# A recurrence's matmuls on one core: block-diagonal pairs of heads become single heads on parts of the array

## The chip, the core and the metric

The kernel runs on one core of a Trainium2 chip. A core has five engines with a queue of instructions each: TensorE (PE in the profile, its weight loads PEld), VectorE (DVE), ScalarE (ACT), GpSimd (POOL) and SyncE (SP), which here only issues transfers. The metric is the device time of one execution in microseconds; lower is better. All arithmetic of the recurrence is float32.

## The reference

```python
# r, k, v, w, a, b: (4 batches, 8 heads, 768 times, 40)
for t in range(S):
    y[:, :, t] = np.einsum('bhd,bhde->bhe', rt, state)
    Sa = np.einsum('bhde,bhe->bhd', state, at)
    state_decay = state * wt[:, :, None, :] - np.einsum('bhd,bhe->bhde', Sa, bt)
    state = state_decay + np.einsum('bhd,bhe->bhde', vt, kt)
x = y.transpose(0, 2, 1, 3).reshape(3072, 320)
x = (1 / (1 + exp(-(x @ w_gate))) * (x @ w_val)) @ w_out          # 320 -> 1536 -> 320
h = x @ w_in                                                      # 320 -> 2048
out = (h * (1 / (1 + exp(-1.702 * h)))) @ w_out2                  # 2048 -> 320
```

Each of the 32 pairs of batch and head has a state of 40 x 40. The two mixtures' weights come as 64-bit words that the kernel decodes on VectorE.

## The kernel before

The 768 times are cut into 24 chunks of C = 32, and a chunk into two halves: a half chunk h (48 of them) is one chunk's work for 16 of the 32 heads. Inside a chunk the recurrence becomes matrix products, with one triangular 32 x 32 inverse for each head; the state passes from one chunk to the next. Two threads, `chain(0)` and `chain(1)`, carry the two halves of the heads along.

Heads go in pairs on the 128 rows: a pair has D + D = 80 rows where dimensions lie on rows, and 32 + 32 where times do. A product for two heads at once needs one operand that is block diagonal, with zeros where one head's rows meet the other's columns. So several operands are written twice, each copy masked for one head:

- `fronts(h)`: running products of w (`wx`, `suf`), then `kb` (k and b scaled; four VectorE or GpSimd instructions, L673), `dd`, and a scaled in place (L705). `diagonal` writes a into `abd` as two masked copies on ScalarE (L743).
- `back(h)`: transposes of `kb` into `pt` (two blocks of four, L771), copied with masks to `kn` (L774); `pm`, the scores between a and k, b (L789). `nl` (L798) and `lk` (L804) are what lies below and above their diagonals. `nl` goes through memory to `solve`, which makes the inverse `tn` on GpSimd (for the first three chunks on VectorE).
- `inverses` and `later` mask `tn` and `lk` into `tb` (L886) and `lkb` (L952); `later` also has `pv` (L938), the scores between v and r.
- `chain`: `po` from the state `sd` (16 passes), copied to `xh`; `pr` from `lkb`, then from `abd` and `xh`; copied to `rs`; `pu` from `tb` and `rs`, masked into `vu` (L1041); `kn` times `vu` added into `po`; the new state through `xb` (L1051), the transposes `px` (L1057) and a ScalarE copy into `sd`. y is read out of `po` (L1076).

`mm` (L561) is a helper through which most matmuls go, so that rows of very different blocks have one line; their tiles' names tell them apart. A float32 matmul of the program is two passes, each with a weight load, in the trace; a transpose and the mixtures' matmuls (in a shortened float32, fp32r) are one.

The first mixture (`moe1`) takes 256 tokens at a time (`gv`, then `xa`), as soon as the chunks are stored, and fills TensorE between the blocks of the recurrence; the second (`ph`, `y`) follows when the recurrence and the first are over. Most transfers are issued by SP.

The order of the instructions on every engine is fixed when the program is built. A planner (`Plan`) steps threads that `yield` an engine and a cost in microseconds, and gives each engine's next place to the thread that could start first, ties by a key. "EITHER" work goes to VectorE or GpSimd, whichever it finds free sooner. On the chip each engine runs its list in that order, waiting on semaphores.

Of the kernel before, what the change touches and what calls it, by code (L numbers as in the profile page):

```python
# [9 lines left out]
F32 = mybir.dt.float32  # L10
# [10 lines left out]
R = 2 * D  # L21
# [9 lines left out]
C_ID, C_I2, C_HM80, C_HM128, C_STR, C_UM, C_LKM, C_NHM, C_SEL, C_END = 0, 128, 168, 170, 172, 204, 276, 340, 342, 374  # L31


def constants():
    k = np.zeros((128, C_END), np.float32)
    p = np.arange(128)
    k[p, C_ID + p] = 1.0
    k[p[:R], C_I2 + p[:R] % D] = 1.0
    for j in range(2):
        k[:R, C_HM80 + j] = p[:R] // D == j  # L40
        k[:R, C_NHM + j] = -k[:R, C_HM80 + j]
        k[:, C_HM128 + j] = (p // C) % 2 == j
    k[p, C_SEL + p % 32] = 1.0
    t = np.arange(C)
    k[:, C_STR : C_STR + C] = t[None, :] < (p % C)[:, None]
    later = (t[None, :] > (p % C)[:, None]).astype(np.float32)
    k[:, C_UM : C_UM + C] = later
    k[:, C_UM + C : C_UM + C + D] = 1.0
    for j in range(2):
        k[:, C_LKM + C * j : C_LKM + C * j + C] = later * k[:, C_HM128 + j : C_HM128 + j + 1]  # L50
    return k
# [11 lines left out]
def layout(inp):  # L63
# [4 lines left out]
    def heads_on_rows(x):  # L68

        y = x.reshape(2, 2, 4, 2, NCH, C, D)  # L70
        return np.ascontiguousarray(y.transpose(4, 0, 3, 6, 1, 2, 5)).reshape(2 * NCH, R, 8, C)

# [5 lines left out]
    def apart(x):  # L78
# [8 lines left out]
        "rt": heads_on_rows(inp["r"]),  # L87
        "vt": heads_on_rows(inp["v"]),
# [120 lines left out]
def program(ctx: ExitStack, tc: tile.TileContext, abkw, rt, vt, vn, cst, x2, x4, in_r, in_k, in_v, in_w, in_a, in_b, moe_w_gate,  # L209
# [18 lines left out]
    ident = k[:R, C_ID : C_ID + R]  # L228
    hm80 = k[:R, C_HM80 : C_HM80 + 2]
    nhm80 = k[:R, C_NHM : C_NHM + 2]  # L230
    hm128 = k[:, C_HM128 : C_HM128 + 2]
    strict = k[:, C_STR : C_STR + C]
    umask = k[:, C_UM : C_UM + C + D]
    lkm = k[:, C_LKM : C_LKM + 2 * C].rearrange("p (j t) -> p j t", j=2)
# [162 lines left out]
    xs_slots, gv_slots, xa_slots, xz_free = Slots(2), Slots(2), Slots(1), Event()  # L397
# [178 lines left out]
    sd = at.tile([R, 16, R], F32, name="sd")  # L576
    ring = 2
    r72s = [at.tile([R, 8, C + D], F32, name=f"r72_{i}") for i in range(ring)]
    vbds = [at.tile([R, 8, 2, C], F32, name=f"vbd_{i}") for i in range(ring)]
    for i in range(2):  # L580
        r72s.append(wpool.tile([R, 8, C + D], F32, tag=f"B{6 + 3 * i}", name="r72_0"))
        vbds.append(wpool.tile([R, 8, 2, C], F32, tag=f"B{7 + 3 * i}", name="vbd_0"))
# [15 lines left out]
    half, tns = {}, {}  # L598
    groups = [[c] for c in range(min(SINGLE, NCH))] + [[c, c + 1] for c in range(SINGLE, NCH, 2)]
# [3 lines left out]
    s_slots, nl_slots, u_slots, tn_slots, tb_slots, b_slots, po_slots = Slots(2), Slots(2), Slots(2), Slots(1), Slots(2), Slots(0), Slots(1)  # L603
    yt_slots, xh_slots, rs_slots = Slots(1), Slots(2), Slots(1)
    e_ab, e_front, e_diag, e_scored, e_stored, e_wc = ([Event() for _ in range(NH)] for _ in range(6))
    e_b, e_vu, e_tb, e_sd, e_y, e_rows = ([Event() for _ in range(NH)] for _ in range(6))
    e_lower, e_tn = ([Event() for _ in range(NCH)] for _ in range(2))
# [25 lines left out]
    def fronts():  # L633

        thread = plan.current
        for h in range(NH):
# [29 lines left out]

            kb = at.tile([R, 4, 4, 2, C], F32, tag="kb", name="kb", bufs=2)
            kbv = kb.rearrange("p g (o x) j t -> p g o x j t", o=2)

            def scaled(eng, x, src, o):  # L670
                sv, cv = (bass.AP(tensor=y.tensor, offset=y[:, o : o + 1].offset, ap=[list(y.ap[0]), [2 * y.ap[1][0], 4], [0, 2], [1, C]])
                          for y in (src, ws))
                eng.tensor_mul(kbv[:, :, o, x ^ o], sv, cv)  # L673
# [13 lines left out]
            on = yield "EITHER", 0.34, 0.12, None, 0.7  # L687
            if h < START:
                ad = wpool.tile([R, 24, C], F32, tag=f"X{8 + h}", name="ad0")
            else:  # L690
                ad = at.tile([R, 24, C], F32, tag="ad", name="ad")
            dd = ad[:, 16:]
# [4 lines left out]
            wc = at.tile([R, 8, 2], F32, tag="wc", name="wc", bufs=DEPTH)  # L697
            nc.vector.tensor_mul(wc, wx[:, :, C:E].broadcast_to([R, 8, 2]), hm80.unsqueeze(1).broadcast_to([R, 8, 2]))
# [5 lines left out]
            on = yield "EITHER", 0.34, None, None, 0.7  # L704
            either[on].tensor_mul(a, a, dd)  # L705
            plan.start(diagonal(h, a, ad), f_key(h), plan.done + plan.LATENCY)
            for o in range(2):
                on = yield "EITHER", 0.34, None, None, 0.7
                scaled(either[on], 1, b, o)
# [5 lines left out]
            plan.start(over(h), f_key(h))  # L715
            plan.start(back(h, kb, ad), f_key(h), plan.done + plan.LATENCY)

    def over(h):

        yield e_front[h]  # L720
        yield e_diag[h]
        plan.done = max(e_front[h].time, e_diag[h].time)
        if h >= START:
            plan.give(ab_slots)
        elif all(e.time is not None for e in e_diag[:START]):
            plan.set(w1ready[1])
# [4 lines left out]
    def kl_parts(kl):  # L731
        return kl[:, : 16 * D].rearrange("p (g j d) -> p g j d", g=8, j=2), kl[:, 16 * D :].rearrange("p (g t) -> p g t", g=4)

    def views(h, ad, kl):
        st = half[h]
        st["abd"], st["dd"] = ad[:, 0:16].rearrange("p (g j) t -> p g j t", j=2), ad[:, 16:]
        st["kn"], st["lk"] = kl_parts(kl)

    def diagonal(h, a, ad):
        abd = ad[:, 0:16].rearrange("p (g j) t -> p g j t", j=2)  # L740
        for j in range(2):
            yield "ACT", 0.4
            nc.scalar.activation(abd[:, :, j, :], a, AF.Copy, scale=nhm80[:, j : j + 1])  # L743
        plan.set(e_diag[h], plan.LATENCY)

    def back(h, kb, ad):
# [3 lines left out]
        abd = ad[:, 0:16].rearrange("p (g j) t -> p g j t", j=2)  # L750
        if h >= START:
            yield kl_slots
            kl = at.tile([128, 16 * D + 4 * C], F32, tag="kl", name="kl")
        else:
            kl = wpool.tile([128, 16 * D + 4 * C], F32, tag=f"X{12 + h}", name="kl0")
            views(h, ad, kl)
        kn, lk = kl_parts(kl)
        st["kl_d"] = drp.tile([128, 16 * D + 4 * C], F32, tag="kl_d", name="kl_d", bufs=DEPTH)
        st["ad_d"] = drp.tile([R, 24, C], F32, tag="ad_d", name="ad_d", bufs=DEPTH)
        rows_done = Event()  # L760

        def on_rows():

            for sb in range(2):
                yield s_slots
                yield "PE", 0.28
                pt = ps_s.tile([128, 4, 2, D], F32, tag="s", name="pt")
                for i in range(4):
                    gi = 4 * sb + i
                    src = kb[:, gi // 2, 2 * (gi % 2) : 2 * (gi % 2) + 2].rearrange("p x j t -> p (x j t)")  # L770
                    nc.tensor.transpose(pt[:, i].rearrange("p j e -> p (j e)"), src, ident)  # L771
                for j in range(2):
                    yield "ACT", 0.28
                    nc.scalar.activation(kn[:, 4 * sb : 4 * sb + 4, j, :], pt[:, :, j, :], AF.Copy, scale=hm128[:, j : j + 1])  # L774
                plan.give(s_slots)
            plan.set(rows_done)

        plan.start(on_rows(), f_key(h) + 0.5, plan.done + plan.LATENCY)
        yield e_diag[h]
        yield s_slots  # L780
        yield "PE", 0.62

        pm = ps_s.tile([128, 4, 2, C], F32, tag="s", name="pm")
        for g2 in range(4):
            for o in range(2):

                a0 = kb[:, g2, 3 * o, 0, :]
                rhs = bass.AP(tensor=a0.tensor, offset=a0.offset, ap=[list(a0.ap[0]), [64 if o == 0 else -64, 2], [1, C]])
                nc.tensor.matmul(pm[64 * o : 64 * o + 64, g2], lhsT=abd[:, 2 * g2 + o].rearrange("p j t -> p (j t)"), rhs=rhs,  # L789
                                 start=True, stop=True)  # L790
        if q == 0:
            yield nl_slots
            nls[c] = at.tile([128, 8, C], F32, tag="nl", name="nl", bufs=2)
# [3 lines left out]
        yield "DVE", 0.2, plan.LATENCY  # L797
        nc.vector.tensor_mul(nls[c][:, hs], pm[:, :, 1, :], strict.unsqueeze(1).broadcast_to([128, 4, C]))  # L798
        if q == 0:
            plan.set(e_lower_first[c])  # L800
        else:
            plan.start(scores_out(c), f_key(h) - 0.3, plan.done + plan.LATENCY)
        yield "DVE", 0.2
        nc.vector.transpose(out=lk, in_=pm[:, :, 0, :])  # L804
        plan.give(s_slots)
# [18 lines left out]
    def scores_out(c):  # L824
# [4 lines left out]
        nc.sync.dma_start(out=ldrs[cs][c - cs[0]].rearrange("g r s -> r g s"), in_=nls.pop(c))  # L829
# [7 lines left out]
    def solve(cs, ldr, eng):  # L837
# [32 lines left out]
        tn = at.tile([128, 8 * len(cs), C], F32, tag="tn", name="tn")  # L870
# [4 lines left out]

    def inverses():

        thread = plan.current
        for h in range(NH):
            thread.key = h - 0.2  # L880
            c, hb = h // 2, h % 2
            yield e_tn[c]
            yield tb_slots
# [667 lines left out]
```

## Time and profile before

| | |
|---|---|
| median of 3 runs | 1319.49 us (1317.58 to 1319.65) |
| profiled execution | 1315.4 us, its span on the core 1313.6 us |
| mean granted TensorE clock | 0.943 |
| busy: TensorE, its weight loads | 1194.1 us (91%), 1100.4 us (84%) |
| busy: VectorE, ScalarE, GpSimd | 865.2 us (66%), 536.1 us (41%), 456.7 us (35%) |
| transfers | 163.31 MB on SP's queue, 126 GB/s in the mean |

A busy share is a mean over stages with different limits, and each stage has to be read for itself. A granted clock of 1.0 is 2.4 GHz, 0.5 is 1.2 GHz; the profile shows the mean of a stretch. Times of rows count from the span's start. "TensorE busy" counts a pass from its start to the end that the profile models for it, so neighbouring passes overlap in it.

### The profile page before, as it was taken

The numbers are of one execution on the slowest core, as the hardware profiler recorded it, in microseconds if no ns is written. First come the engines' busy times: TensorE is split into PE (matmuls) and PEld (weight loads), VectorE is DVE, ScalarE is ACT, GpSimd is POOL, SyncE is SP. The second block draws the span as 40 slices with busy tenths as digits, with TensorE's granted clock in tenths as the row PEclk, the third lists the DMA queues.
The fourth block names the chain that finished last, engine by engine and source line by source line (L and its number), as shares of the span: only waits on it lengthen the run. The fifth ranks groups of instructions, "written<-read, shape, count | busy, mean of one in ns | idle before, by whom it ended". The sixth has DMA issues, their size and how long they took to land. (4 is left out here: it accounts for less than half of the span.)

```text
span 1313.6 us, 30246 instructions
## 1 busy us (share of the span) xinstructions
PE 1194.1 (91%) x11505; PEld 1100.4 (84%) x11505; DVE 865.2 (66%) x2298; ACT 536.1 (41%) x1354; POOL 456.7 (35%) x882
## 2 busy tenths in 40 slices
PE   4366885999999999999999999999999999999996
PEld 3355784889889898999899999999988798899995
DVE  8997897756476656566656444439998656556552
ACT  3233454234434344444344433337774243434332
POOL 3236487836371808181817270002341000000000
PEclk9975795699999999999999999999999999999999
DMA  6566776475646474656465543225533422222110
GB/s 166 139 175 170 178 211 174 134 174 146 158 115 175 128 178 132 167 143 174 136 135 163 121 127 86 73 58 153 150 107 97 114 87 55 88 59 79 45 43 23
DMA packets 245144, 165.31 MB, mean 126 GB/s; under 512 B 173504, under 2 KB 215680, under 8 KB 244992
## 3 DMA queue, kind: packets, MB, share of 16 engines
q1 hardware_dynamic: 244992, 163.31, 47.4%
q8 instruction: 93, 1.52, 0.5%
q14 instruction: 59, 0.48, 0.1%
HBM read 117.05 MB, written 46.20 MB: 124 GB/s over the span
## 5 line engine op out<-in xcount | busy, mean ns | idle before, releaser
L561 PE MATMUL gv<-xs,w1i 128*128 128x256 f32 x1728 | 271.2, 299 | 0.0
L561 PEld LDWEIGHTS gv<-xs,w1i 128*128 128x128 f32 x1728 | 228.9, 196 | 7.1
L561 PE MATMUL y<-w2o,g 128*128 128x320 f32 x1152 | 185.2, 309 | 3.8 <-DVE g L1308 2.3
L859 POOL TENSOR_TENSOR ut<-x,u 128x126 f32<-128x126 f32 (+27 forms) x341 | 158.4, 465 | 83.7 <-DMA x<-in_x_dram 50.2
L561 PEld LDWEIGHTS y<-w2o,g 128*128 128x128 f32 x1152 | 176.2, 188 | 12.7 <-DVE g L1308 3.1
L561 PE MATMUL xa<-g,w1o 128*128 128x256 f32 x1152 | 173.1, 288 | 2.2 <-DVE x L464 1.7
L561 PE MATMUL ph<-xs,w2i 128*128 128x512 f32 x672 | 172.5, 396 | 2.4 <-DVE gg L1300 2.4
L862 POOL TENSOR_TENSOR x<-x,ut 128x126 f32<-128x126 f32 (+27 forms) x341 | 148.4, 435 | 26.0
L561 PEld LDWEIGHTS xa<-g,w1o 128*128 128x128 f32 x1152 | 151.4, 192 | 4.6 <-DVE x L464 1.9
L561 PEld LDWEIGHTS ph<-xs,w2i 128*128 128x128 f32 x672 | 122.9, 189 | 25.6 <-DVE gg L1300 4.3
L506 DVE TENSOR_TENSOR sg<-gv,sg 128x256 f32<-128x256 f32 x144 | 60.3, 419 | 112.7 <-ACT sg L504 112.1
L504 ACT ACTIVATE sg<-gv 128x256 f32<-128x256 f32 x144 | 55.3, 384 | 174.3 <-PE gv L561 173.4
L1300 DVE TENSOR_TENSOR gg<-ph,sg 128x512 f32<-128x512 f32 x96 | 66.0, 688 | 52.9 <-ACT sg L1296 52.8
L1306 ACT CAST g<-gg 128x512 fp32r<-128x512 f32 x96 | 59.5, 620 | 96.1 <-DVE gg L1300 96.0
L1308 DVE TENSOR_TENSOR g<-gg,g 128x512 fp32r<-128x512 f32 x96 | 66.7, 695 | 43.5 <-ACT g L1306 43.3
L1296 ACT ACTIVATE sg<-ph 128x512 f32<-128x512 f32 x96 | 57.2, 596 | 92.8 <-PE ph L561 92.7
L511 ACT CAST g<-sg 128x256 fp32r<-128x256 f32 x144 | 58.1, 404 | 88.5 <-DVE sg L506 75.3
L774 ACT ACTIVATE kl<-pt,k 128x160 f32<-128x160 f32 x192 | 67.3, 391 | 53.2 <-PE pt L771 39.5
L673 DVE TENSOR_TENSOR kb<-ab,suf 80x256 f32<-80x256 f32 x158 | 81.9, 552 | 3.8 <-PE pt L771 3.8
L561 PE MATMUL gv<-xs,w1r 128*128 128x256 f32 x288 | 82.8, 307 | 0.0
L513 DVE TENSOR_TENSOR g<-sg,g 128x256 fp32r<-128x256 f32 x144 | 64.7, 449 | 21.7 <-ACT g L511 21.4
L771 PE MATMUL pt<-k,kb 80*128 80x80 f32 x384 | 54.1, 270 | 25.7 <-DVE kb L673 12.9
(123 smaller groups left out, 2056.9 us busy)
## 6 DMA issues: line engine op xcount, KB each, us to landing
kl_d<-kl SPq DMA_DIRECT2D x44, 384.0 KB
kl_l<-kl_d SPq DMA_DIRECT2D x44, 384.0 KB
ab<-in_abkw_dram SPq DMA_DIRECT2D x44, 322.8 KB
ad_d<-ad SPq DMA_DIRECT2D x44, 240.0 KB
ad_l<-ad_d SPq DMA_DIRECT2D x44, 240.0 KB
u<-ldr SPq DMA_DIRECT2D x20, 256.0 KB
w<-in_moe_w_out_dram SPq DMA_DIRECT2D x32, 160.0 KB
w<-in_moe_w_in_dram SPq DMA_DIRECT2D x32, 128.0 KB
```

The lines of the kernel that those rows point to most:

```text
L506: nc.vector.tensor_mul(gg, gv[:, 1, :], gg)
L511: nc.scalar.copy(out=g4[:, 0], in_=gg)
L513: nc.vector.tensor_sub(out=g4[:, 1], in0=gg, in1=g4[:, 0].bitcast(F32))
L561: nc.tensor.matmul(o, lhsT=w, rhs=x, start=start, stop=stop, skip_group_check=True)
L673: eng.tensor_mul(kbv[:, :, o, x ^ o], sv, cv)
L774: nc.scalar.activation(kn[:, 4 * sb : 4 * sb + 4, j, :], pt[:, :, j, :], AF.Copy, scale=hm128[:, j : j + 1])
L859: eng.tensor_mul(tv, x[:, :n, s : s + 1].broadcast_to([128, n, m]), u[:, s + 1 :, s].unsqueeze(1).broadcast_to([128, n, m]))
L862: eng.tensor_add(x[:, :n, s + 1 :], x[:, :n, s + 1 :], tv)
L1296: nc.scalar.activation(sg, ph, AF.Sigmoid, scale=1.702)
L1300: nc.vector.tensor_mul(gg, ph, sg)
L1306: nc.scalar.copy(out=g4[:, 0], in_=gg)
L1308: nc.vector.tensor_sub(out=g4[:, 1], in0=gg, in1=g4[:, 0].bitcast(F32))
```

## The change

Nothing is block diagonal any more. A head has 40 of 64 rows (J = 64; R = 112 rows hold a pair), and each product is one matmul for one head, on a part of the array that its rows and its columns name: 64 or 32 rows by 64 or 32 columns. Four heads that follow each other in the list `HEADS` lie on four different parts. The masked copies fall away: `abd`, `lkb`, `tb`, the four `kb` writes (now two), `diagonal`, `inverses`. `pt` and `px` are ordinary matmuls with an identity, not transposes; `px` lies in unused columns of `po`'s PSUM banks. `kn` times `vu` is added in two blocks, `added(0)` and `added(1)`, each for the rows of `vu` that are ready. `sd` holds 40 columns where it held 80, `kl` 448 where it held 768. The loads are padded from 80 to 112 rows. PSUM banks of `po` are cleared once at the start.

```diff
+J = 64
+R = 112
...
+    HEADS = [(2 * g2 + o, g2, o, j) for g2 in range(4) for o in range(2) for j in range(2)]
+
+    def dims(j):
+        return slice(J * j, J * j + D)
+
+    def times(o, j):
+        return slice(64 * o + C * j, 64 * o + C * j + C)
...
             def kb0():
-                for o in range(2):
-                    on = yield "EITHER", 0.34, None, None, 0.7
-                    scaled(either[on], 0, kk, o)
+                on = yield "EITHER", 0.45, None, None, 0.8
+                either[on].tensor_mul(kb[:, :, 0], kk, ws)
...
-            for sb in range(2):
-                yield s_slots
-                yield "PE", 0.28
-                pt = ps_s.tile([128, 4, 2, D], F32, tag="s", name="pt")
-                for i in range(4):
...
+            yield s_slots
+            yield "PE", 0.4
+            pt = ps_s.tile([128, 8, D], F32, tag="s", name="pt")
+            for gi, g2, o, j in HEADS:
+                for x in range(2):
+                    mm(pt[times(o ^ x, j), gi], kb[dims(j), gi, x], ident[j], True, True)
+            yield "ACT", 0.42
+            nc.scalar.copy(out=kn, in_=pt)
...
+        for gi, g2, o, j in HEADS:
+            mm(pm[times(o, j), g2], an[dims(j), gi], kb[dims(j), gi].rearrange("p x t -> p (x t)"), True, True)
...
+            at_ = dims(j ^ o)
+            mm(pv[times(o, j), g2], vt_[at_, gi], r72[at_, gi, 0:C], True, True)
...
-                for i in range(4):
-                    mm(po[sb][:, i], sd[:, 8 * hb + 4 * sb + i], r72[:, 4 * sb + i], i == 0, False)
...
+            for gi, g2, o, j in HEADS:
+                mm(po[o][dims(j), g2], sd[dims(j ^ o), 8 * hb + 4 * o + g2], r72[dims(j ^ o), gi], g2 == 0, False)
...
+            def added(u):
+
+                for gi, g2, o, j in HEADS:
+                    rows = times(o ^ u, j)
+                    mm(po[o][dims(j), g2], kn[rows, gi], vuo[rows, g2, o], False, u == 1)
...
-                mm(pr[rows, g2], lkb[rows, g2].rearrange("p j t -> p (j t)"), vu[rows, gi], gi < 2, False)
...
+                mm(pr[rows, g2], lk[rows, g2], vuo[rows, g2, o], g2 == 0, False)
...
+                mm(pr[times(o, j), g2], an[dims(j), gi], xh[o][dims(j), g2], False, True)
...
+            yield "PE", 0.55
+            added(0)
...
-                mm(pu[dst, g2], tb[rows, g2].rearrange("p j t -> p (j t)"), rs[rows, g2], gi < 2, True)
...
+                mm(pu[times(1 - o, j), g2], tns[c][times(o, j), 4 * hb + g2], rs[times(o, j), g2], g2 == 0, True)
...
+                for gi, g2, o, j in HEADS:
+                    mm(pxs[o][dims(j ^ o), g2], xb[o][dims(j), g2], ident[j], True, True)
...
+            yield "PE", 0.55
+            added(1)
```

Two places of the orders show what it moves. TensorE, a half chunk in the middle of the program (h = 20 or so), before: a row gives the line, tile written and tiles read, the output's rows and columns, and how many matmuls of the program follow each other.

```order
L561 MATMUL xa<-g_6158,w1o 128x256 x8
L1057 MATMUL px<-k,xb 80x80 x4
L771 MATMUL pt<-k,kb 128x80 x4
L561 MATMUL gv<-xs,w1i 128x256 x10
L561 MATMUL po<-r_0_86,sd 80x72 x8
L561 MATMUL pr<-vu,lkb 64x72 x8
L771 MATMUL pt<-k,kb 128x80 x4
L561 MATMUL gv<-xs,w1i 128x256 x2
L561 MATMUL pr<-xh,ad_l 64x72 x8
```

The same place in the changed program (`mm` is now L557):

```order
L557 MATMUL xa<-g_8074,w1o 128x256 x3
L557 MATMUL po<-r_0_86,sd 40x72 x16
L557 MATMUL xa<-g_8074,w1o 128x256 x5
L557 MATMUL pm<-kb,ad 32x64 x16
L557 MATMUL gv<-xs,w1i 128x256 x8
L557 MATMUL pr<-vu,kl_l 32x72 x16
L557 MATMUL pr<-xh,ad_l 32x72 x16
L557 MATMUL po<-vu,kl_l 40x72 x16
L557 MATMUL gv<-xs,w1i 128x256 x4
```

Every block of the recurrence has 16 matmuls of half the rows where it had 8, dense matmuls now stand between `po` and `pr`, and the first `kn` block follows `pr`. For one half chunk the changed order has, in this stretch, seven groups of divided blocks with dense matmuls on both sides: `po` with `pm`, the three above, `pv`, `pt`, `pu`, the second `kn` block and `px`. Over the program 3440 matmuls of the recurrence become 8416; counted in passes, 128 a half chunk become 352.

VectorE, the first half chunk of the program, before:

```order
L652 SCALAR_TENSOR_TENSOR wx<-w_100,ones 80x264
L658 SCALAR_TENSOR_TENSOR suf<-w_100,ones 80x264
L663 TENSOR_SCALAR iw<-wx 80x8
L664 RECIPROCAL iw<-iw 80x8
L693 TENSOR_TENSOR ad_126<-wx,iw 80x256
L698 TENSOR_TENSOR wc<-wx,k 80x16
L705 TENSOR_TENSOR ab_105<-ab_105,ad_126 80x256
L673 TENSOR_TENSOR kb<-ab_105,suf 80x4x64 x2
```

And in the changed program:

```order
L1068 MEMSET po 128x512 x4
L660 SCALAR_TENSOR_TENSOR wx<-w_104,ones 112x264
L666 SCALAR_TENSOR_TENSOR suf<-w_104,ones 112x264
L671 TENSOR_SCALAR iw<-wx 112x8
L672 RECIPROCAL iw<-iw 112x8
L692 TENSOR_TENSOR ad_138<-wx,iw 112x256
L697 COPY wc<-wx 112x8
L704 SCALAR_TENSOR_TENSOR ad_138<-ab_111,ad_138 112x256
L706 TENSOR_TENSOR kb<-ab_111,suf 112x8x32
```

`kb` is half as much, and the clears of PSUM are new. Up to the 32nd and last weight decode of the first mixture (`w`) VectorE's order has 45 of `kb` before and 20 in the changed program, and as many `xb` (16) and `nl` (16) in both.

## Rows read from the trace of the kernel before

**Rows 1.** Busy time of each engine by stretch (count of instructions in brackets).

```profile
core 0: us, PE busy (x) PEld busy (x) DVE busy (x) ACT busy (x) POOL busy (x), PEclk, DMA share, GB/s
20.00:100.00 80.00, 42.52 (x449) 36.94 (x448) 78.95 (x287) 26.92 (x72) 24.64 (x30) 0.89 0.64 156
100.00:220.00 120.00, 93.01 (x960) 83.46 (x959) 100.78 (x267) 49.43 (x138) 79.42 (x151) 0.70 0.69 182
220.00:300.00 80.00, 71.05 (x743) 64.96 (x743) 51.72 (x135) 30.42 (x84) 50.77 (x106) 0.76 0.64 159
300.00:860.00 560.00, 547.30 (x6615) 514.22 (x6611) 323.55 (x848) 221.34 (x592) 250.73 (x523) 0.99 0.55 138
```

**Rows 2.** VectorE's groups, 0 to 220 us: busy us, mean ns | idle before.

```profile
L673 DVE TENSOR_TENSOR kb<-ab,suf 80x256 f32<-80x256 f32 x45 | 23.6, 553 | 0.0
...
L258 DVE TENSOR_SCALAR w<-w 128x384 int32<-128x384 int32 (+1 forms) x32 | 12.6, 399 | 2.1 <-DMA w<-in_moe_w_out_dram 2.0
...
L1051 DVE TENSOR_TENSOR xb<-po,wc 80x320 f32<-80x320 f32 x16 | 7.4, 475 | 0.0
...
L798 DVE TENSOR_TENSOR nl<-pm,k 128x128 f32<-128x128 f32 x16 | 4.5, 281 | 2.3 <-PE pm L789 2.1
...
L952 DVE TENSOR_TENSOR lkb<-kl_l,k 128x256 f32<-128x256 f32 x3 | 1.5, 485 | 0.1
```

**Rows 3.** TensorE in order of time, 499.9 to 517.5 us: start, length, block.

```profile
499.94 0.88 PE L561 MATMUL xa<-g,w1o 128*128 128x256 f32 x6
500.75 0.72 PE L561 MATMUL pu<-rs,tb 64*64 64x72 f32 x16
501.39 0.50 PE L561 MATMUL xa<-g,w1o 128*128 128x256 f32 x2
501.83 0.66 PE L938 MATMUL pv<-r,vbd 80*64 80x32 f32 x16
502.41 1.21 PE L561 MATMUL gv<-xs,w1i 128*128 128x256 f32 x8
503.46 1.30 PE L561 MATMUL po<-vu,kl_l 128*80 128x72 f32 x16
504.57 0.72 PE L561 MATMUL gv<-xs,w1i 128*128 128x256 f32 x4
505.12 0.28 PE L561 MATMUL gv<-xs,w1r 128*128 128x256 f32 x1
505.24 0.28 PE L561 MATMUL gv<-xz,w1r 128*128 128x256 f32 x1
...
506.65 0.69 PE L789 MATMUL pm<-kb,ad 80*64 80x64 f32 x16
507.27 1.70 PE L561 MATMUL gv<-xs,w1i 128*128 128x256 f32 x12
...
510.56 0.44 PE L1057 MATMUL px<-k,xb 80*80 80x80 f32 x4
510.83 0.44 PE L771 MATMUL pt<-k,kb 80*128 80x80 f32 x4
...
512.34 1.30 PE L561 MATMUL po<-r,sd 80*80 80x72 f32 x16
513.57 0.72 PE L561 MATMUL pr<-vu,lkb 64*64 64x72 f32 x16
514.22 0.50 PE L771 MATMUL pt<-k,kb 80*128 80x80 f32 x4
514.51 0.48 PE L561 MATMUL gv<-xs,w1i 128*128 128x256 f32 x2
...
517.19 0.72 PE L561 MATMUL pu<-rs,tb 64*64 64x72 f32 x16
```

**Rows 4.** The same, from 500.74 to 500.80 and from 500.90 to 500.97 us alone.

```profile
500.75 0.28 PE L561 MATMUL pu<-rs,tb 64*64 64x72 f32 x2
500.75 0.41 PE L561 MATMUL pu<-rs,tb 64*64 64x72 f32 x6
```

More of the change, by code (lines that the diff above doesn't have):

```diff
@@ L703, in fronts @@
                 plan.give(wc_slots)
[L704 to L709, printed above, removed]
+            yield "DVE", 0.4
+            nc.vector.scalar_tensor_tensor(out=ad[:, 0:8], in0=a, scalar=-1.0, in1=dd, op0=ALU.mult, op1=ALU.mult)
+            on = yield "EITHER", 0.45, None, None, 0.8
+            either[on].tensor_mul(kb[:, :, 1], b, ws)
             end = plan.done
@@ L714, in fronts @@
             plan.set(e_front[h], plan.LATENCY)
-            plan.start(over(h), f_key(h))
+            if h >= START:
+                plan.give(ab_slots)
+            elif h == START - 1:
+                plan.set(w1ready[1])
             plan.start(back(h, kb, ad), f_key(h), plan.done + plan.LATENCY)
[L718 to L726, printed above, removed]
     def f_key(h):
         return max(h - (F0 if h < FH else FLAG), h / 100)
-    def kl_parts(kl):
-        return kl[:, : 16 * D].rearrange("p (g j d) -> p g j d", g=8, j=2), kl[:, 16 * D :].rearrange("p (g t) -> p g t", g=4)
+    KL = 8 * D + 4 * C
     def views(h, ad, kl):
         st = half[h]
[L736 to L744, printed above, removed]
+        st["an"], st["dd"] = ad[:, 0:8], ad[:, 8:]
+        st["kn"] = kl[:, : 8 * D].rearrange("p (g d) -> p g d", g=8)
+        st["lk"] = kl[:, 8 * D :].rearrange("p (g t) -> p g t", g=4)
     def back(h, kb, ad):
@@ L874, in solve @@
             plan.set(e_tn[c])
[L876 to L883, printed above, removed]
-            on = yield "EITHER", 0.34, None, None, 0.7
-            tb = at.tile([128, 4, 2, C], F32, tag="tb", name="tb", bufs=2)
-            either[on].tensor_mul(tb, tns[c][:, 4 * hb : 4 * hb + 4].unsqueeze(2).broadcast_to([128, 4, 2, C]),
-                                 hm128.unsqueeze(1).unsqueeze(3).broadcast_to([128, 4, 2, C]))
-            half[h]["tb"] = tb
-            if c == group_of[c][-1] and hb:
-                plan.give(tn_slots)
-            plan.set(e_tb[h])
     def preps():
@@ L1016, in chain @@
[L1016 to L1022 removed]
+            for gi, g2, o, j in HEADS:
+                rows = times(o, j)
+                mm(pr[rows, g2], lk[rows, g2], vuo[rows, g2, o], g2 == 0, False)
@@ L1023, in chain @@
+            for o in range(2):
+                yield ex[o]
+            yield "PE", 0.55
+            for gi, g2, o, j in HEADS:
+                mm(pr[times(o, j), g2], an[dims(j), gi], xh[o][dims(j), g2], False, True)
+            plan.give(xh_slots)
+            prs.append(plan.done + plan.LATENCY)
+            yield "PE", 0.55
+            added(0)
+            plan.done = prs.pop()
+            thread.ready, thread.engine = plan.done, None
             yield rs_slots
@@ L1064, in chain @@
-            for sb in range(2):
-                yield "PE", 0.54
-                for gi, g2, o, s2, i in groups8:
-                    if s2 == sb:
-                        mm(po[sb][:, i], kn[:, gi].rearrange("p j e -> p (j e)"), vu[:, gi], False, True)
-                if nxt:
-                    plan.start(state(sb), h, plan.done + plan.LATENCY)
+                for o in range(2):
+                    yield "DVE", 0.28
+                    xb.append(at.tile([R, 4, D], F32, tag="xh", name="xb", bufs=4))
+                    nc.vector.tensor_mul(xb[o], po[o][:, :, C:], half[h + 2]["wc"][:, o::2].broadcast_to([R, 4, D]))
@@ new lines, in state @@
+                yield "PE", 0.35, plan.LATENCY
+                for gi, g2, o, j in HEADS:
+                    mm(pxs[o][dims(j ^ o), g2], xb[o][dims(j), g2], ident[j], True, True)
+                plan.give(xh_slots)
+                for o in range(2):
+                    yield "ACT", 0.25
+                    nc.scalar.copy(out=sd[:, 8 * hb + 4 * o : 8 * hb + 4 * o + 4], in_=pxs[o])
+                    plan.set(es[o], plan.LATENCY)
+            yield "PE", 0.55
+            added(1)
+            if nxt:
+                plan.start(state(), h, plan.done + plan.LATENCY)
@@ L1096, in chain @@
                     yield e
-    passed = []
+    passed, used, prs = [], {}, []
     e_set = [Event() for _ in range(2)]
     def set_up():
+        yield "DVE", 2.4
+        for pair in banks:
+            for bank in pair:
+                nc.vector.memset(bank, 0.0)
         yield "POOL", 0.6
```

236 lines of the change are left out of this document (89 added, 147 removed).

## Prediction

> **What bounds the kernel now.** I read the busy times by stretch first [rows 1]. From 300 to 860 us TensorE is busy 547.30 of 560 us at a granted clock of 0.99, its upper level (2.4 GHz): there the time is TensorE's work, and any change of that work counts in full. Ahead of that it is not so: from 20 to 100 us VectorE is busy 78.95 of 80 us and TensorE 42.52; from 100 to 220 us VectorE has 100.78 of 120, TensorE 93.01, at a clock of 0.70, which is a mix of the levels of 1.2 and 2.4 GHz; from 220 to 300 us neither is full. So there are two sums to make: VectorE's work in the first 220 us, and TensorE's work for one half chunk in the stretch that TensorE bounds. After the recurrence only the second mixture of experts is left, which the change does not touch.
>
> VectorE's groups up to 220 us [rows 2] show what the masks cost: kb is written 45 times at 553 ns, xb 16 times at 475 ns, and lkb and nl are smaller. The first step of the first mixture's weight decodes (w) stands 32 times there, all there are, so 220 us is about where that decoding ends.
>
> TensorE in order of time [rows 3] shows one half chunk of the recurrence among the dense matmuls. The reader should take the time from one block's start to the next one's start. pu comes back after 16.44 us (500.75 to 517.19); 560 us hold 34 such periods. A dense matmul takes 0.12 us (505.12 to 505.24). The recurrence's f32 matmuls run as two passes each, so 8 of the program are 16 here. pu: 0.64 us (500.75 to 501.39). pv: 0.58 (501.83 to 502.41). pm: 0.62 (506.65 to 507.27). pr: 0.65 (513.57 to 514.22). po, which uses the whole array: 1.11 (503.46 to 504.57) and 1.23 (512.34 to 513.57). A px of four: 0.27 (510.56 to 510.83), a pt of four 0.29 (514.22 to 514.51). For one half chunk: po 2.34, pr twice 1.30, pu 0.64, pv 0.58, pm 0.62, px twice 0.54, pt twice 0.58: 6.60 us.
>
> Two more things stand there. First, po's 16 passes come one by one, 69 ns each, but pu's come two at a time: two have begun by 500.80 and six by 500.97 [rows 4], and 16 passes of the same 72 columns take 0.64 us, not 1.11. Two halves of the array do work at once. Second, a change between dense and divided blocks costs: six dense xa from 499.94 to 500.75 take 0.81 where six of 0.12 would take 0.72, so 0.09 on the way in; two from 501.39 to 501.83 take 0.44, of which 0.24 is work and 0.09 the next way in, so 0.11 on the way back. After a block on the whole array it is less: four in 0.55 (504.57 to 505.12), 0.07 over.
>
> **TensorE after the change.** A block of 8 pair matmuls becomes one of 16 head matmuls: 32 passes, which name four parts of the array in turn. If four parts work at once as two do now, that is 8 rounds of four where pu has 8 rounds of two, and a round lasts as long as its columns: the price of a 72-column block is pu's, 0.64 us. Six blocks of a half chunk have 72 columns: po from the state, pr twice, pu, and kn into po twice (that product is split in two by which vu half is ready): 3.84 us. pm keeps its 64 columns and 8 rounds: 0.62. pv has 32 columns but half as many weight columns; between 0.32 (half of pu) and its 0.58 I take 0.5. px has 40 columns in 8 rounds: between 0.36 (pu's by columns) and 0.64, take 0.45. pt becomes 32 ordinary matmuls of 40 columns, 16 rounds: 16 x 0.08 x 40/72 = 0.71, at most 1.28; take 0.7. Sum 6.11 us, against 6.60. In the order the new half chunk has 7 stretches of divided blocks between dense ones, where the trace's half chunk has four, and four returns from whole-array blocks fall away: 3 x 0.20 - 4 x 0.07 = 0.3 us more. So 0.2 us less for a half chunk, and over 34 of them about -6 us. The margin is thin: the 352 passes are taken at 6.11/352 = 17.4 ns each, and at 19 ns the gain of this part and that of the next are both used up.
>
> So the gain that the words of the change suggest (four at a time, not two) is not there: the number of matmuls doubles, and blocks that had two halves at work keep their 8 rounds. po gains, the split kn gives it back, and pt gets dearer.
>
> **VectorE before 220 us.** The order has the same 32nd weight decode after 20 kb in place of 45, and the lkb and tb ahead of it are gone. 25 kb x 0.553 = 13.8 us; lkb 1.5 more; xb falls from 320 to 160 columns, between 475 ns (no gain) and half of it: take 0.31, 16 x 0.165 = 2.6; wc becomes a copy of half its columns, taken at nothing. nl doubles from 281 ns; with kb's 256 columns as the upper bound, 16 x 0.14 to 0.27, take 2.2 us more. The four clears of PSUM stand ahead of the first load's arrival and cost nothing unless they last longer than that load. Net about 16 us less. What of it shortens the program? In 20 to 100 us all of it, in 100 to 220 us only where VectorE ends the wait: 100.78 of 120. Both bounds, 0 and 16, stay for the range; I take 10. ScalarE loses its two masked copies of a and half of kl's copies, and GpSimd its lkb and tb; neither is full in any stretch [rows 1], so that is taken at nothing.
>
> **Sum.** -10 and -6 on the profiled execution (1315.4 us, span 1313.6) give about 1299; the median of the runs is 1319.49, 4 us higher, so about 1304 for a median.
>
> **Rivals.**
> *TensorE can't begin passes that fast (slower).* Place: every divided block. The densest stretch of the trace is pv, 16 passes in 0.58 us, 36 ns each; nothing there shows one at 17 ns over a block. At 36 ns, 352 passes take 12.7 us, 6.4 with the changeovers more than now, over 34 half chunks 218 us: 1530. It decides from 19 ns on. For it: twice the passes and twice the weight loads. Against it: two of pu's begin within 50 ns, long before either is over [rows 4], so the start itself is not what takes 36. The Trainium skill, page "TensorEngine Tiling (Array Packing)", section Performance Considerations (Instruction Overhead), speaks against this change: a matmul has some 60 cycles of overhead, and one should not take a tiling factor from a dimension that is already small. As an estimate from that page, 60 cycles at 2.4 GHz are 25 ns, 352 of them 8.8 us, 2.5 more a half chunk with the changeovers: some 1395. No row here shows a pass that short, so the trace neither bears it out nor excludes it.
>
> *Parts that share columns don't work at once (slower).* po from the state, both kn, and px put two or four row parts over the same columns; the trace has only parts with columns of their own. If they go two by two, each takes what po takes now, 1.11 in place of 0.64, and px 0.54: 1.5 us more a half chunk, 51 us: about 1355.
>
> *Nothing comes of it (no change).* TensorE's -0.2 us turns out as +0.1 and the early VectorE work was covered by the chain of the first halves: 1317 to 1322.
>
> *More comes early.* All 16 us count, and since TensorE then has less to wait for between 100 and 300 us, where its clock is at 0.70 and 0.76, part of that stretch comes back at the upper level; and the 13 us that it idles from 300 to 860 us shrink: 1275 to 1293.
>
> **How the numbers follow.** Forecast (1294 to 1316) 0.47; more early 0.13; nothing 0.10; shared columns 0.14; slow starts, wholly or partly, 0.16. From 1280 to 1400 holds all but the far part of the last (0.13) and a little of the second (0.04). Two tenths of a per cent are about what the measurement tells from no change. Faster: nearly all of the first two, 0.57; within: 0.10; slower: 0.33.
>
> **What would show it.** Right: in the stretch that TensorE bounds, pu, pr and each po block at 0.60 to 0.70 us for 32 passes, pt about 0.7, a half chunk again near 16.2 us, and VectorE's last weight decode some 10 us earlier than 220. Wrong: blocks near 0.9 or above (slow starts), or only po and px above 1 us (shared columns); blocks under 0.5 us would make it faster than forecast, as would a half chunk under 15.5 us. If VectorE is less busy early and the first dense matmuls come no earlier, the early relief was covered.

## The result, and the profile after

| | before | after |
|---|---|---|
| median | 1319.57 us (1317.58 to 1321.58) | 1271.91 us (1270.67 to 1275.54) |
| ratio | | 0.9643 [0.9619, 0.9668] |
| profiled execution, span | 1315.4, 1313.6 us | 1272.3, 1270.5 us |
| TensorE busy, passes | 1194.1 us, 11505 | 1167.5 us, 22209 |
| VectorE, ScalarE busy | 865.2, 536.1 us | 773.5, 440.9 us |

The change took 47.7 us off, where 15 were forecast. The same stretches as in [rows 1], after:

```profile
core 0: us, PE busy (x) PEld busy (x) DVE busy (x) ACT busy (x) POOL busy (x), PEclk, DMA share, GB/s
20.00:100.00 80.00, 44.78 (x1492) 37.10 (x1496) 74.25 (x283) 14.83 (x42) 17.15 (x21) 1.00 0.69 173
100.00:220.00 120.00, 95.04 (x2344) 81.51 (x2335) 96.94 (x267) 38.86 (x112) 82.76 (x155) 0.82 0.72 188
220.00:300.00 80.00, 73.86 (x1965) 64.49 (x1964) 43.96 (x124) 21.19 (x58) 54.59 (x119) 0.89 0.57 146
300.00:860.00 560.00, 557.68 (x13964) 494.60 (x13964) 269.92 (x779) 179.26 (x494) 233.97 (x483) 1.00 0.52 133
```

From 300 to 860 us TensorE's idle time fell from 12.7 to 2.3 us, and more was done: 2602 dense matmuls of the first mixture, where before had 2429, and 35 half chunks' pu, where before had 34. TensorE in order of time, against [rows 3] (start, length, block):

```profile
499.61 0.70 PE L557 MATMUL pr<-vu,kl_l 32*32 32x72 f32 x32
500.24 0.70 PE L557 MATMUL pr<-xh,ad_l 40*32 40x72 f32 x32
500.88 0.71 PE L557 MATMUL po<-vu,kl_l 32*40 32x72 f32 x32
501.52 0.50 PE L557 MATMUL gv<-xs,w1i 128*128 128x256 f32 x2
501.95 0.46 PE L557 MATMUL pv<-r,vt 40*32 40x32 f32 x32
502.33 0.50 PE L557 MATMUL gv<-xs,w1i 128*128 128x256 f32 x2
...
505.01 0.80 PE L557 MATMUL pt<-k,kb 40*32 40x40 f32 x64
505.74 1.70 PE L557 MATMUL gv<-xs,w1i 128*128 128x256 f32 x12
...
510.21 0.52 PE L557 MATMUL po<-k,xb 40*40 40x40 f32 x32
510.66 1.46 PE L557 MATMUL gv<-xs,w1i 128*128 128x256 f32 x10
...
516.04 0.70 PE L557 MATMUL pr<-vu,kl_l 32*32 32x72 f32 x32
```

From start to start, pr and po are 0.63 or 0.64 us, pt 0.73, px 0.45: the prices of the prediction; pv, taken at 0.5, is 0.38. The half chunk (pr to pr) is 16.43 us here, as in [rows 3], but one alone says little: from pu of h = 20 to pu of h = 40 the mean is 16.44 us before and 15.92 here, and in the runs with another number of the planner (below) 15.9 to 16.1 in both kernels.

VectorE's groups to 220 us, against [rows 2]:

```profile
L254 DVE TENSOR_SCALAR w<-w 128x384 int32<-128x384 int32 (+1 forms) x32 | 13.4, 419 | 9.9 <-DMA w<-in_moe_w_gate_dram 4.2 <-DMA w<-in_moe_w_out_dram 3.5 <-POOL w1i L278 2.0
...
L706 DVE TENSOR_TENSOR kb<-ab,suf 112x256 f32<-112x256 f32 x15 | 7.0, 470 | 0.0
...
L772 DVE TENSOR_TENSOR nl<-pm,k 128x256 f32<-128x256 f32 x17 | 7.0, 410 | 0.4 <-PE pm L557 0.3
...
L1016 DVE TENSOR_TENSOR xb<-po,wc 112x160 f32<-112x160 f32 x16 | 4.6, 312 | 0.9 <-PE po L557 0.8
...
L679 DVE TENSOR_TENSOR kb<-ab,suf 112x256 f32<-112x256 f32 x6 | 3.1, 512 | 0.0
```

kb went from 23.6 to 10.1 us, xb from 7.4 to 4.6, nl from 4.5 to 7.0: what the prediction had. VectorE now waits 9.9 us ahead of the decodes, 7.7 of them for loads. The last of the 32 in the row stands at 211.9 us (before 219.3), the first mixture's first output matmul (xa) at 136.9 (before 158.9).

Early on the blocks' lengths tell of the clock what the profile's clock does not:

```profile
83.35 1.18 PE L557 MATMUL pr<-xh,ad 40*32 40x72 f32 x32
84.47 1.20 PE L557 MATMUL po<-vu,kl 32*40 32x72 f32 x32
85.59 0.70 PE L557 MATMUL pv<-r,vt 40*32 40x32 f32 x32
...
159.74 1.20 PE L557 MATMUL po<-vu,kl_l 32*40 32x72 f32 x32
```

The same block takes 1.12 us here, 1.75 times as long, though 20 to 100 us shows a granted clock of 1.00; po's row is as long as the last one's, in a stretch recorded at 0.5 (155.6 to 193.1 us). The clock's record begins at 135.1 us after and at 74.8 before; what stands ahead of it ran at 1.2 GHz by these lengths. So the 0.89 of [rows 1], like the 1.00 above, isn't the clock of that stretch.

To compare, I count TensorE's busy time ahead of the second mixture at its upper clock: busy time in stretches at 0.5, and ahead of the first record, counts half. What is left of the time is idle, or the other half ("slow"). (A block above takes 1.75 times as long, not twice. By that factor the work would be 10 us more before and 9 after, and the difference almost the same.)

| us | second mixture begins | work at 2.4 GHz | slow | idle |
|---|---|---|---|---|
| before | 946.1 | 774.4 | 69.8 | 101.9 |
| after | 905.1 | 755.7 | 63.0 | 86.5 |

From here on "the second 256 tokens begin" with the first output matmul (xa) of the first mixture's second 256 tokens: at 281.3 us before, 255.9 after. Ahead of that the work fell from 129.7 to 116.7 us; behind it by 5.8.

### The profile page after: what moved, and what is told of

It reads as the page before. It is cut to its first block, busy times and chain, and to the rows that moved or that the text cites. A ratio compares the mean times of both kernels' runs of the same rounds, so it can differ in the third digit from the quotient of the medians.

```text
span 1270.5 us, 51101 instructions
## 1 busy us (share of the span) xinstructions
PE 1167.5 (92%) x22209; PEld 1038.1 (82%) x22209; DVE 773.5 (61%) x2142; ACT 440.9 (35%) x1114; POOL 434.5 (34%) x846
## 4 chain that ended last, share of the span: by engine, by line
PE 77%; DVE 8%; DMA 6%; POOL 4%; issue 2%; SPq 2%; ACT 0%; POOLq 0%; DVEq 0%; ACTq 0%
PE gv L557 23%; PE ph L557 12%; PE y L557 12%; PE xa L557 10%; PE po L557 8%; PE pr L557 4%; PE pt L557 2%; PE pu L557 2%; POOL ut L834 2%; POOL x L837 2%; PE pm L557 2%; PE pv L557 1%; DMA x<-in_x_dram 1%; DVE ut L834 1%; DMA w<-in_moe_w_gate_dram 1%
## 5 line engine op out<-in xcount | busy, mean ns | idle before, releaser
L557 PE MATMUL gv<-xs,w1i 128*128 128x256 f32 x1728 | 275.0, 300 | 1.9 <-DVE xs L425 1.3
L557 PEld LDWEIGHTS gv<-xs,w1i 128*128 128x128 f32 x1728 | 229.2, 196 | 18.2 <-issue 2.0
L834 POOL TENSOR_TENSOR ut<-x,u 128x126 f32<-128x126 f32 (+27 forms) x341 | 163.7, 480 | 175.7 <-DMA x<-in_x_dram 141.7
L557 PE MATMUL y<-w2o,g 128*128 128x320 f32 x1152 | 186.1, 310 | 3.1 <-DVE g L1272 2.4
L557 PEld LDWEIGHTS y<-w2o,g 128*128 128x128 f32 x1152 | 177.1, 189 | 11.9 <-DVE g L1272 3.5
L557 PE MATMUL xa<-g,w1o 128*128 128x256 f32 x1152 | 179.5, 292 | 2.1 <-ACT g L507 1.8
L557 PE MATMUL ph<-xs,w2i 128*128 128x512 f32 x672 | 171.2, 394 | 1.9 <-DVE gg L1264 1.9
L837 POOL TENSOR_TENSOR x<-x,ut 128x126 f32<-128x126 f32 (+27 forms) x341 | 152.3, 447 | 25.5 <-POOL ut L834 0.2
L557 PEld LDWEIGHTS xa<-g,w1o 128*128 128x128 f32 x1152 | 153.0, 193 | 9.1 <-ACT g L507 2.0
L557 PEld LDWEIGHTS ph<-xs,w2i 128*128 128x128 f32 x672 | 122.7, 189 | 24.0 <-DVE gg L1264 2.8
L557 PE MATMUL gv<-xs,w1r 128*128 128x256 f32 x288 | 82.0, 304 | 0.0
L557 PE MATMUL gv<-xz,w1r 128*128 128x256 f32 x288 | 77.1, 286 | 0.0
L897 DVE TENSOR_TENSOR vu<-pv,k 64x128 f32<-64x128 f32 x96 | 27.6, 287 | 73.4 <-PE pv L557 72.4
L1004 DVE TENSOR_TENSOR vu<-pu,k 64x288 f32<-64x288 f32 x96 | 43.7, 455 | 41.6 <-PE pu L557 39.1
```

What stands on the lines that cost most here:

```text
L557: nc.tensor.matmul(o, lhsT=w, rhs=x, start=start, stop=stop, skip_group_check=True)
L834: eng.tensor_mul(tv, x[:, :n, s : s + 1].broadcast_to([128, n, m]), u[:, s + 1 :, s].unsqueeze(1).broadcast_to([128, n, m]))
L837: eng.tensor_add(x[:, :n, s + 1 :], x[:, :n, s + 1 :], tv)
L1004: nc.vector.tensor_mul(vuo[rows, :, o, :], pu[rows], umask[rows].unsqueeze(1).broadcast_to([64, 4, C + D]))
```

## The experiments

**VectorE's work put back.** Theory V: VectorE's relief made the early gain. Theory P: the shorter blocks on the chain did.

```
 either[on].tensor_mul(kb[:, :, 0], kk, ws)     # and kb[:, :, 1], xb[o]
+either[on].tensor_mul(kb[:, :, 0], kk, ws)     # the same
...
+for eng in (nc.vector, nc.gpsimd):             # for lkb, tb
+    eng.tensor_mul(more, strict..., strict...)
```

> The changed kernel with the vector work of the masks put back, in the old places and with the order on every engine as it was: both kb writes and both xb writes of a half chunk are done twice, and two masked copies of 256 columns (lkb, tb) go to a scratch tile, one on VectorE and one on GpSimd. That is some 2 to 2.5 us more on VectorE for a half chunk, 40 to 50 us over the 20 half chunks ahead of 256 us. Theory V (VectorE's relief ahead of 256 us gave the 25 us that the changed kernel is ahead by then): most of them go again, 1287 to 1300 us. Theory P (the matmul blocks on the recurrence's chain became shorter, above all at TensorE's lower clock, and VectorE's relief is mostly covered): 1272 to 1280 us.

Measured: 1305.9 us, all but 14 of the gain gone. The rows of this run (windows), and TensorE's waits in the last window:

```profile
0.00:265.00 265.00, 177.67 (x4913) 152.16 (x4914) 232.97 (x695) 65.46 (x183) 153.87 (x273) 0.89 0.66 171
265.00:936.00 671.00, 647.68 (x15377) 576.26 (x15378) 399.39 (x1133) 223.66 (x629) 318.45 (x630) 0.99 0.51 130
```

```profile
PE po L557 <- DVE yt L1042: 12.8, 16, 1.9
PE pr L557 <- issue: 2.7, 2, 2.0
PE xa L557 <- ACT g L507: 1.8, 1, 1.8
```

The changed kernel's, 256 us to the same point:

```profile
0.00:256.00 256.00, 177.12 (x4913) 151.48 (x4913) 204.12 (x636) 65.71 (x183) 132.33 (x247) 0.89 0.68 178
256.00:905.00 649.00, 641.40 (x15376) 572.55 (x15377) 337.07 (x991) 223.95 (x629) 280.27 (x571) 0.99 0.52 134
```

The second 256 tokens begin 9 us later, and the stretch behind is 22 us longer, although VectorE is busy only 399 of 671 us: 16 times TensorE stands at a px (the timeline has "po" from xb) for VectorE; the row names yt, the instruction right behind xb in VectorE's queue. VectorE's sum to the second mixture, 632 us, is that of before (635). (The expectation's 20 half chunks are those whose `fronts` are done by 256 us; the chain has done 11.)

The same, with the planner told of each instruction (another yield ahead of it); then told, but without them:

> As the run with the vector work put back, which took 1305.9 us, but now the planner is told of each added instruction, as it was of the masks before, and orders around them (it may give one to GpSimd). If that run's loss is the work itself: again 1295 to 1310 us, with some 8 us of it ahead of the second block of positions and the rest in waits of TensorE for VectorE among the dense matmuls. If it is an order that didn't know of the work: 1275 to 1290 us.

> The counterpart of the run in which the planner was told of the vector work put back (1305.1 us): here it is told of the same instructions, and orders around them, but they are not issued. So the order is that one's, the work the changed kernel's. If the order alone costs what that run lost: 1295 to 1305 us. If the loss is VectorE's work, and any fair order would do: 1270 to 1282 us.

Measured: 1305.1 us (ten runs, 1297.9 to 1316.4) and 1286.8 us. So of the 33 us, 15 come with the order and 18 with the work. That the 15 are room made for the work is not shown: another order alone costs the changed kernel 13 us further down. The rows of the run with the work planned for:

```profile
0.00:286.00 286.00, 180.58 (x5041) 155.65 (x5042) 234.99 (x702) 66.50 (x183) 146.13 (x271) 0.68 0.63 163
286.00:940.00 654.00, 638.70 (x15249) 572.81 (x15248) 411.06 (x1166) 224.41 (x629) 299.24 (x591) 0.99 0.51 131
```

There the loss stands early: the second 256 tokens begin at 286 us (before 281), and only 654 us lie behind. By TensorE's account this run has less work than the changed kernel (749.3 us; its order goes to the divided array 271 times, the changed kernel's 309) and 120.7 us of idle.

Parts of it, first kb alone, then without kb:

> The changed kernel with only kb written twice (the masks' largest item on VectorE, 25 of its writes in the first 220 us; off the recurrence's chain). If the early gain is VectorE's time and the later one waits on the chain: the first output matmul 5 to 8 us later than at 136.9 us, and after 256 us little more: 1277 to 1284 us. If any vector work costs among the dense matmuls too: 1288 to 1296 us.

> The changed kernel with only the rest of the vector work put back, without kb: both xb writes done twice, and the two masked copies to scratch tiles (one on VectorE, one on GpSimd), order unchanged; with kb too it was 1305.9 us, with kb alone 1283.9. If what costs time after 256 us are the writes that stand on the recurrence's chain (xb, and what queues behind the copies): 1288 to 1296 us, nearly all of it after 256 us. If vector work only costs ahead of 256 us: 1276 to 1281 us.

Measured: 1283.9 and 1285.9 us: 12 and 14, together 8 less than both at once. For kb 8 us arise ahead of the second 256 tokens and 5 behind, for the rest 4 and 10. So each costs most where its theory puts it, and something in the other place too.

ScalarE's share, and the other direction, in the kernel before (kb's second copies left out):

```
+nc.scalar.copy(out=more, in_=ad[:, 0:8])  # twice; kn's copy twice
...
-eng.tensor_mul(kbv[:, :, o, x ^ o], sv, cv)
+eng.tensor_mul(kbv[:, :, o, x ^ o, 0], sv, cv)
```

> The changed kernel with ScalarE's mask work put back: two copies of a (256 columns) to a scratch tile and kn's copy twice, 1.4 us more on ScalarE for a half chunk, order unchanged. If ScalarE's relief gave part of the gain: 1277 to 1285 us. If it was covered, as the prediction took it: 1270 to 1275 us.

> The kernel before, its matmuls as they were, with each write of kb halved: of the two copies that kb keeps of every k and b column (one for each head of the pair), only the first is written, the other stays zero from two clears at the start, so the recurrence's results lack the second head's part. The planner is told of the shorter writes. Some 45 writes ahead of 220 us at 0.3 us in place of 0.55 are about 10 us less for VectorE. Theory V (VectorE's time ahead of the first outputs comes through): the first output matmul 8 to 12 us earlier than at 158.9 us, 1303 to 1312 us. Theory P (the matmul blocks are what the early part waits for): 1316 to 1321 us.

Measured: 1270.5 us, nothing; and 1313.2 us, ratio 0.994 [0.992, 0.996]. There the first output matmul came 7 us earlier, the second 256 tokens no earlier. The time lies between both theories, 6 to 8 us under before. As the planner was told, the order is another one too, and such a change alone moves this kernel by more (below): this run decides nothing.

**TensorE's blocks.** More TensorE work on the chain; then matmuls that nobody needs, for the clock:

```
-for gi, g2, o, j in HEADS: mm(po[o]..., sd..., r72..., g2 == 0, False)
+for _ in range(2 if h < 20 else 1):  # the same block twice
...
+yield "PE", 0.22                     # a thread with the last key
+nc.tensor.matmul(pf, ones, ones)     # 64 x 256, until the first xa
```

> The changed kernel with the product of state and r72 into po issued twice for the first 20 half chunks (the second one starts the accumulation afresh, so the result is the same): 32 more passes, 1.1 us at the lower clock, 0.64 at the upper, which is about what this block lost against before. Theory P: the block is on the chain of both heads' halves, so 10 to 20 of these prices come through: 1281 to 1292 us. Theory V: TensorE has time to spare ahead of 256 us, so 1272 to 1277 us.

> The changed kernel with some 270 matmuls of ones on a PSUM tile that nobody reads, issued where the planner leaves TensorE idle ahead of the first mixture's first output matmul (they change the planner's order a little). They are meant to bring TensorE's clock up before 135 us, where the changed kernel's blocks take 1.1 us for 32 passes, 28 ns each, as at 1.2 GHz. Theory P with the clock as lever: blocks of 0.64 us from early on, the first outputs 5 to 15 us earlier, 1257 to 1268 us. Theory V: TensorE's speed isn't what the first 135 us wait for, and the extra matmuls only get in the way: 1272 to 1282 us.

Measured: 1278.9 and 1306.5 us. Some 11 of the 20 doubled blocks lie ahead of the second 256 tokens, which begin at 256 us as without them; the others cost 7 us, 9 x 0.64 and a little, where TensorE is full. That is against theory P. The filler brought the clock up from 7 us on, and blocks of 0.64 us, but TensorE was then busy 80.00 of 80 us from 20 to 100, its own work came late, and the first output matmul at 171 us in place of 137. The dose was too large, and the order another one, to say what the clock alone is worth.

The order of the heads, `for o, for j, for g2` in place of `for g2, for o, for j`:

> The changed kernel with the 16 head matmuls of every block in another order: all four of one part of the array, then the next part's, where the change names the four parts in turn. If passes run in the order given, and one part's wait for each other (36 ns each, as the 16 of pv before): a block of 72 columns 1.15 us in place of 0.64, some 3.5 to 4 us more a half chunk, 1390 to 1410 us. If the parts take what is theirs from the queue whatever stands between: no change, 1268 to 1276 us.

Measured: 1618.9 us, far above both. A block in this run:

```profile
605.71 1.52 PE L557 MATMUL pu<-rs,tn 32*32 32x72 f32 x32
607.17 0.98 PE L557 MATMUL gv<-xs,w1i 128*128 128x256 f32 x6
```

It takes 1.46 us, where 1.15 was expected. On one part passes start 62 ns apart, so 8 of them are 0.50 us; four parts named in turn start 32 in that time, a round of four every 62 ns, and 0.13 us more pass until the next block. Named part after part, four passes of this block last 245 ns, the others 221, as the first four of a block do where the parts come in turn: I read them as the parts' first passes. They begin 0.28 us apart, so a part begins when the one ahead of it has begun five of its eight. Neither theory has that: the parts reach a few passes ahead, no further. Another run has it by name. With the filler, pv stands behind pm in the program, and begins ahead of pm's last six passes:

```profile
29.17 0.58 PE L556 MATMUL pm<-kb,ad 40*32 40x64 f32 x26
29.54 0.21 PE L556 MATMUL pv<-r,vt 40*32 40x32 f32 x1
29.54 0.22 PE L556 MATMUL pm<-kb,ad 40*32 40x64 f32 x1
29.55 0.21 PE L556 MATMUL pv<-r,vt 40*32 40x32 f32 x1
29.55 0.26 PE L556 MATMUL pm<-kb,ad 40*32 40x64 f32 x3
```

The Trainium skill, page "TensorE: Matmul & The Clock Gate", section "Part 3: Packing small matmuls — row/col tiling", says that matmuls start and end in the order of the program. These starts don't agree with that; on the ends, which the profile models, no run here shows anything.

Fewer changes between divided and dense matmuls: pt and pm issued together if two PSUM places are free; then the planner stays with divided blocks.

```
+if s_slots.free:  # both places: pt, then pm, in one step
...
+parts = [x for x in best[engine] if x[3] is None and x[1] <= first + wait]
+if self.kind is None and parts: ready = parts   # wait: 0, or 0.2 us
```

> The changed kernel with pt and pm of a half chunk issued together where two PSUM places are free, so that TensorE goes to the divided array once for both; in the planner's order the stretches of divided blocks fall from 309 to 249 for the whole recurrence. If a way in and back costs 0.2 us as the prediction read it: 60 x 0.2 = 12 us less, most of it among the dense matmuls, 1258 to 1264 us. If it costs nothing (the blocks' prices hold all): 1270 to 1276 us.

> The run with pt and pm together (1262.6 us) with one rule more in the planner: after a block on parts of the array it takes another such block ahead of a dense one, if one is ready by then. In its order the stretches of divided blocks fall from 249 to 217. With 0.2 us for a way in and back: 32 x 0.2 = 6 us less, 1254 to 1259 us, if the dense matmuls that stand back delay nothing.

> The same rule, with TensorE allowed to wait up to 0.2 us for the next such block, and the planner told the blocks' measured lengths (0.64 us for a block of 72 columns, not 0.55; 0.72 for pt, 0.45 for px, 0.38 for pv). The stretches fall to 177. At 0.2 us each 72 fewer are 14 us less than the 1262.6 us of the run with pt and pm together; waits that come true take some of it back: 1246 to 1258 us. If chain blocks that stay behind one another make the results late: 1262 to 1270 us.

Measured: 1262.6 us, ratio to before 0.957 [0.953, 0.961], the fastest of all; 1278.0; 1334.3. For the first, TensorE's work to the second mixture is 743.7 us: 12.0 less for 60 stretches, 0.2 us each, as the prediction had read it. With the planner's rule the work falls further, to 736.1 us (7.6 for 32 stretches) and, where it may wait, 734.1 (2.0 for 40 more), but idle rises from 92.0 to 102.4 and 140.6. It may be that dense matmuls no longer fill the waits of the chain; that these are worse orders for another reason isn't excluded, and the last run was also told the measured lengths, which alone cost 13 us (below). The Trainium skill, page "TensorEngine Tiling (Array Packing)", section "Key Properties", says that a change of tiling drains TensorE; the 0.2 us agree.

**Orders that mean nothing.** One planner number in each kernel, `LATENCY = 0.55` or `0.43` for 0.49; and in the changed one the blocks' measured lengths as costs.

> The kernel before with the same number moved, 0.55 in place of 0.49. If orders as such matter little: within 6 us of 1319. If the old kernel had an order that happened to be bad: 1300 to 1312 us.

> The changed kernel with one number of the planner moved: the latency that it assumes between two engines is 0.55 us in place of 0.49. No work changes, only the order. If the gain of 48 us is the change's: within 6 us of 1272. If a good part of it is an order that happened to suit: 1280 to 1295 us.

> The kernel before with the planner's latency at 0.43 us (0.49 as it stands, 1319.5 us; 0.55: 1294.8 us). If the order of before was one bad draw: 1290 to 1302 us. If its orders scatter: anything from 1290 to 1325, and 1312 to 1322 as likely as not. If the work alone decides between the kernels, less than 1294.8 never shows.

> The changed kernel with the planner's latency at 0.43 us (0.49: 1271.9 us; 0.55: 1268.2 us). If the change is worth the 26 us that the pair at 0.55 shows, it stands 20 to 33 us under its partner, most likely 1266 to 1285 us. If it is worth the full 48: 40 us or more under its partner.

> The changed kernel with the planner told the measured lengths of TensorE's blocks (0.64 us for 72 columns in place of 0.55; pt 0.72 in place of 0.40; px 0.45 for 0.35; pv 0.38 for 0.50). If an order laid out by true lengths waits less: 1262 to 1270 us. If the order's quality doesn't hang on them: 1270 to 1285 us.

| planner's latency, us | 0.43 | 0.49 | 0.55 |
|---|---|---|---|
| before | 1301.5 | 1319.6 | 1294.8 |
| after | 1272.6 | 1271.9 | 1268.2 |
| difference | -28.9 | -47.7 | -26.5 |

With measured costs: 1284.9 us, 13 more; knowing more was no help. Of its three orders the kernel before has the worst. Its windows, and those of its run with 0.55 (to the first output matmul, the second 256 tokens, the second mixture):

```profile
0.00:159.00 159.00, 94.24 (x950) 82.61 (x951) 139.17 (x455) 54.77 (x145) 67.13 (x126) 0.79 0.66 166
159.00:281.00 122.00, 99.79 (x1022) 89.99 (x1020) 93.00 (x234) 48.65 (x138) 82.37 (x149) 0.75 0.67 171
281.00:946.00 665.00, 650.07 (x7616) 614.00 (x7616) 402.64 (x1094) 282.39 (x772) 286.75 (x584) 0.99 0.53 136
```

```profile
0.00:158.00 158.00, 92.99 (x933) 81.35 (x933) 138.03 (x451) 55.32 (x146) 66.49 (x125) 0.92 0.64 162
158.00:257.00 99.00, 80.90 (x889) 75.16 (x887) 81.19 (x201) 42.73 (x125) 76.93 (x132) 0.83 0.70 190
257.00:924.00 667.00, 658.66 (x7769) 622.17 (x7768) 413.31 (x1119) 284.65 (x784) 306.28 (x614) 0.99 0.55 140
```

The same kernel, without a change of work, comes to its second 256 tokens 24 us earlier. That is what the change seemed to gain by then. At 0.55 the changed kernel is 15 us ahead of its partner at that point, at 0.43 not at all; the first output matmul alone comes 22 to 24 us earlier at all three settings.

## Why the prediction was wrong

- *Direction and mechanism* held: four parts work at once, also where they share columns (po, px), so both slow rivals fell. The 25 ns a pass that the prediction worked out from the Trainium skill, page "TensorEngine Tiling (Array Packing)", section "Instruction Overhead", don't show across parts: 32 passes in 0.63 us are 20 ns each, pt's 64 in 0.73 us 11, and all of the recurrence's passes behind the second 256 tokens 17 in the mean (213.5 us for 12256).
- *TensorE's sum* looks right and was too small. Between the second 256 tokens and the second mixture the two traces' work differs by -5.8 us, for the -6 forecast: by the same count the recurrence's blocks have 27 less, and the dense matmuls 21 more (`gv` 132 to 139 ns), which is where the changeovers are paid: 269 ways to the divided array and back where before has 165. But that -5.8 meets -6 is in part luck of this pair of orders: at 0.43 and 0.55 the same stretch has 16.6 and 15.8 us less. Over all 48 half chunks, the same work in both kernels, TensorE has 18.7 us less (24.9 and 21.5 at 0.43 and 0.55), where the forecast's 0.2 us for each would be 9.6.
- *TensorE ahead of 300 us* had no term. Its blocks are shorter there as well, with few dense matmuls between them to pay changeovers: 13.0 us less work ahead of the second 256 tokens (8.3 and 5.6 at 0.43 and 0.55). Yet alone this seems to buy nothing: 11 doubled po blocks went in there for nothing.
- *"I take 10"* is the step that failed most, and with it the bound of 16. Putting VectorE's work back costs 34 us in an order that doesn't know of it, and 18 in one that does (1286.8 to 1305.1); both are over the bound. The step counted VectorE up to 220 us alone, as if an engine that is half idle cost nothing behind. There the xb write stands on the recurrence's chain, in a queue with kb and the mixture's work: 22 of the 34 us arose there with the order as it was. With the order that knew of the work, nearly all of it stood early. ScalarE, taken at nothing, was nothing.
- *The order* was a term of the sum that I didn't have. "The order has the same 32nd weight decode after 20 kb in place of 45" I read as the change's doing, and took everything else of it as given. A number that means nothing moves before by 18 to 25 us. So of the 47.7 us, as an estimate from three settings, some 20 are before's own bad order, and 26 to 29 the change's at the two other settings, still 11 to 14 more than the 15 forecast.

The two parts don't add up. Over the three settings the second mixture begins 33.7 us earlier in the mean, of which TensorE's work is 21.7, idle 6.3 and slow time 5.6 (one profile each). With VectorE's work put back and planned for, TensorE has its shorter work, and waits instead: 1305.1 us, where the three orders of before have 1305.3 in the mean. I read this as: the shorter blocks come through only since VectorE's relief lets them. It rests on one planned order; no run gives the old blocks all of VectorE's relief.

Open: what the lower clock of the first 135 us costs, and what makes one order better than another; neither the measured costs nor fewer changeovers sorted them. How much of the gain is TensorE's alone is open too.

## What to carry to other kernels

When a program's order comes from a planner, run the kernel before under two or three settings that mean nothing ahead of pricing a change; the scatter is a term of the range, and a comparison of single orders can credit the change with it. Work on a half idle engine isn't free where it stands in one queue with a link of the chain that a full engine waits for. Divided matmuls want their parts named in turn. Their blocks want to stand side by side where that comes free; the two orders here that forced it further were slower.

## What the runs showed of the hardware

- Four parts of 32 to 40 rows do 32 passes of 72 columns in 0.63 us, 20 ns each (inside the block a round of four every 62 ns); pt's 64 of 40 columns in 0.73 us, 11 ns each. Named part after part, pu's 32 take 1.46 us, 46 ns each.
- A part can begin passes ahead of another part's that stand before them in the program (pv ahead of pm's last six, at 29.54 us).
- A change to the divided array and back costs 0.2 us: 12.0 us for 60 of them (with the planner's first rule 7.6 for 32).
- The clock's row reads 1.00 ahead of its first record, where blocks last as at 1.2 GHz (1.12 us, not 0.64).
